# Attention with a gated FFN on one Trainium2 core: one half of scores in each block of six key tiles is exponentiated by GpSimd as a power of e^(1/4)

## The chip, the core and the metric

The kernel runs on one core of one Trainium2 chip. The engines are named as in the profile: PE is TensorE (PEld its weight loads), DVE is VectorE, ACT is ScalarE, POOL is GpSimd and SP is SyncE, which issues DMAs here. The metric is the device time of one execution in microseconds, as the median of several runs.

## The reference

All tensors are float32; the sequence has 2048 tokens of width 512. The input is normalised, and goes into an attention with 32 heads of width 16 and into a SwiGLU FFN of width 1792. The attention's output is multiplied by the SiLU of the FFN's output, and the input is added.

```python
def _A_ref(x, wqkv, wo):
    H = 32; Dh = D // H
    q, k, v = qkv[0], qkv[1], qkv[2]
    scale = Dh ** -0.5
    scores = jnp.einsum("bhqd,bhkd->bhqk", q, k) * scale
    p = _softmax(scores, axis=-1)
    o = jnp.einsum("bhqk,bhkd->bhqd", p, v)
    return (lambda x, *d: x.transpose(*d))(o, 0, 2, 1, 3).reshape(B, S, D) @ wo

def _B_ref(x, w_gate, w_up, w_down):
    g = _silu(x @ w_gate)
    u = x @ w_up
    return (g * u) @ w_down

xn = _layernorm(x, axis=-1)
s = _A_ref(xn, A_wqkv, A_wo)
g = _silu(_B_ref(xn, B_w_gate, B_w_up, B_w_down))
return x + s * g
```

The scale is 16^(-1/2) = 1/4, so the softmax needs exp(score / 4) of 32 x 2048 x 2048 scores.

## The kernel before

**Stages.** A prologue (to about 160 us) normalises the input and makes queries, keys and values. Then the attention and the FFN run interleaved for some 1,200 us, and the output projection ends the kernel.

**Units and blocks.** The attention goes through 32 units: 8 groups of four heads times 4 blocks of 512 queries. Each unit has 16 key tiles of 128 keys. `plan()` (L58) cuts these into 115 blocks of 2 to 6 key tiles, and says for each how many FFN steps stand behind each of its slots. 28 of the blocks have six key tiles and 24 FFN steps.

**Slots.** A key tile has two slots, `j` = 0 and 1, one for each pair of heads, so a block of six has 12 slots, n = 0 to 11. In a slot (L879 to L918) TensorE makes two products of 128 keys by 512 queries (L899), one for each head of the pair. They run side by side on two halves of the rows of the array. In a usual slot both land in the two halves of `score[j]` in PSUM, and one activation of 128x1024 takes the exponential of both into a tile `pr` (L902). In a slot that is `apart` the second half goes to the PSUM bank `spare`, of which there is only one. The slots in `shared` are apart, as is a block's last slot. For a block of six, `shared` is (2, 5, 7, 9, 11) and the FFN steps behind slots 2 to 11 are 1, 3, 3, 2, 3, 2, 2, 3, 1, 4. In a shared slot ScalarE exponentiates one half from PSUM (L910), and VectorE only copies the other half from PSUM to `pr` (L907). That copy goes on the list `kept_back`, and after the block's last slot ScalarE exponentiates all of the list in place (L920). So the five halves of a block of six that VectorE copies out are exponentiated late; the first of them is the second half of slot 2, which lies in the block's second key tile.

**Values.** Behind the first two slots of the next block, `values(prev)` (L418 to L424) multiplies the values with all of the last block's `pr`: four products for each key tile (L423), one for each head, key tile by key tile. TensorE takes its instructions in program order. So the values wait for each half's exponential in turn, and the rest of the block stands behind them.

**FFN steps.** `fill(n)` (L471) draws n steps from the generator `ffn` (L246). One step is a pair of products into the banks `bankx` and `banky` (L237). 24 steps make one tile of hidden features, and in the blocks of six they make exactly one. When a tile begins, behind slot 2, VectorE is given the split of the next gate and up weights into a high and a low part (`split_gu`, L198 a cast and L199 a subtraction, both from SBUF to SBUF), and a third of the way on the split of the next `w_down` rows (`split_wd`, L208 and L209, likewise). When it ends, ScalarE makes a tanh (L264), VectorE two products with it (L265 and L266), and then the split of the result (L230 and L231).

**Order.** The whole order is written out by hand (`tc.manual_schedule()`): each engine takes its instructions in program order, and semaphores are put in where data or buffers need them. GpSimd has constants and a few subtractions in the prologue, DMA issues in between (L243, L450), and two operations for each tile of the output from 1308 us on (`store_out`, L380 to L383, called from L398).

Of the kernel before, what the change touches and what calls it, by code (L numbers as in the profile page):

```python
# [2 lines left out]

# [6 lines left out]
F32 = mybir.dt.float32  # L10
# [3 lines left out]
AF = mybir.ActivationFunctionType  # L14
ALU = mybir.AluOpType
# [4 lines left out]
P = 128  # L20
# [6 lines left out]
TB = S // NB  # L27
# [14 lines left out]
SIZES = (2, 3, 4, 5, 6)  # L42
# [71 lines left out]
def tile_block(ctx: ExitStack, tc: tile.TileContext, x, wqkv, wo, w_gate, w_up, w_down, out):  # L114
# [3 lines left out]
    mm, act, dve, sp, pool = nc.tensor.matmul, nc.scalar.activation, nc.vector, nc.sync, nc.gpsimd  # L118
# [11 lines left out]
    const = ctx.enter_context(tc.tile_pool(name="const", bufs=1))  # L130
# [3 lines left out]

    ident = const.tile([P, P], F32, name="ident")
    make_identity(nc, ident)
    bankx = pone.tile([P, 512], F32, name="bankx")
    banky = pone.tile([P, 512], F32, name="banky")
    banks = (bankx, banky)
# [27 lines left out]
    def load_k(g, c, i=None):  # L167
        load_rows(kst[(g * NB + c) % RING if i is None else i],
                  k_d[:, g * 64:(g + 1) * 64, c * TB:(c + 1) * TB], KSLOT)

    def load_q(u, i=None):
        g, b = divmod(u, NB)
        load_rows(qst[u % 2 if i is None else i], q_d[:, g * 64:(g + 1) * 64, b * TB:(b + 1) * TB], QSLOT)

    def load_shift(u):
        for h in range(2):
            sp.dma_start(qst[u % 2][h * HALF:h * HALF + 2].bitcast(F32),
                         sh_d.rearrange("(s u) (j h t) -> u h s j t", s=2, j=2, h=2)[u, h])

    def load_v(g, c):  # L180
        sp.dma_start(vst[(g * NB + c) % RING], v_d[g][:, c * CT:(c + 1) * CT])
# [38 lines left out]
    def catch_up():  # L220
        while after:
            after.pop(0)()
# [135 lines left out]
    def out_steps():  # L358
        for b in range(NB - 1):
            if b not in stage and (len(queue) <= NB, 0 in stage and now > stage.get(0, now), ready[0] == DT)[b]:  # L360
                for c in range(DT - 1):
                    load_out(b, c)
                stage[b] = now
            if b in stage and b < 2 and (b, 1) not in stage and now > begin[u0 + b]:
                load_out(b, DT - 1)
                stage[b, 1] = now
            if b in stage and (b, 2) not in stage and now > stage[b] and (b < 2 or len(queue) <= 2):
                splits.extend((b, c) for c in range(DT - 1))
                stage[b, 2] = now
                for t in range(0 if b else NT):  # L370
                    load_gates(t)
            if (b, 1) in stage and (b, 5) not in stage and now > stage[b, 1]:
                splits.insert(0 if not b else len(splits), (b, DT - 1))
                stage[b, 5] = now
        for _ in range(min(2, len(splits))):
            b, c = splits.pop(0)
            split_o(lhs[b, c], parts_o[b, c])
            ready[b] += 1
# [39 lines left out]
    def values(item):  # L418
        u, tiles, probs = item
        for i, kt in enumerate(tiles):  # L420
            v = vst[(u // NB * NB + kt // CT) % RING]
            for h in range(4):
                mm(acc[h * 32:h * 32 + DH + 1], v[:, kt % CT, h * (DH + 1):(h + 1) * (DH + 1)],  # L423
                   probs[2 * i + h // 2][:, h % 2], start=kt == 0, stop=kt == KT - 1, skip_group_check=True)  # L424

    def turn_acc(first, last):
        o1 = late.tile([P, TB], F32, tag="o1", name="o1")
        dve.transpose(o1[:, :last - first], acc[:, first:last])
        return o1
# [13 lines left out]
    def finish(u, o1=None):  # L443
        g, b = divmod(u, NB)
        normalise(u, 0, TB, o1=o1)
        if g % 2:
            o2 = late.tile([P, TB], F32, tag="o1", name="o2")
            dve.transpose(o2, on[b])
            if g < NG - 1 or b < 2:
                (pool if g < NG - 1 else sp).dma_start(o_d[g // 2, b], o2)  # L450
            else:
                whole = hh.rearrange("p f j t -> p (f j) t")
                lhs[b, DT - 1] = whole[:, 2 * (DT - 1)], whole[:, 2 * DT - 1]
                split_o(lhs[b, DT - 1], o2)
                ready[b] += 1
# [15 lines left out]
    def fill(n):  # L471
        nonlocal given
        while n > 0 and not blocked():
            next(queue[0][1])
            queue[0][2] -= 1
            if not queue[0][2]:
                queue.pop(0)
            n -= 1
            given += 1
# [14 lines left out]
    with ExitStack() as pro:  # L494
# [53 lines left out]
        def low_w(m):  # L548
            hi, lo = parts_w(m)
            return pool.tensor_sub(lo, wraw[m], hi.bitcast(F32))  # L550
# [117 lines left out]
        for c in range(1, DT):  # L668
            high_w(8 + c)
            part = low_w(8 + c)  # L670
# [190 lines left out]
    exps = []  # L861

    coming = []
    for u in range(units):
        g, b = divmod(u, NB)
        q = qst[u % 2]
        kt = 0
        for now in range(begin[u], begin[u + 1]):
            size, shared, parts = blocks[now]
            ended, kept_back = None, []  # L870
            tiles = range(kt, kt + size)
            kt += size
            probs = []
            if not now:
                fill(FIRST[0])
            if now < 2:
                load_k(0, 2 + now)
                load_v(0, 2 + now)
            for n in range(2 * size):  # L879
                t, j = tiles[n // 2], n % 2  # L880
                if n == 2 and prev and prev[1][-1] == KT - 1:
                    values(prev)
                    if prev[0] < units - 2:
                        ended = prev[0]
                    else:
                        finish(prev[0])
                    catch_up()
                elif n == 2:
                    catch_up()
                    if prev:  # L890
                        values(prev)
                k, kc = kst[(g * NB + t // CT) % RING], t % CT


                room, last_pair = score[j], n == 2 * size - 1
                apart = last_pair or n in shared
                for h in range(2):
                    r = slice(h * HALF, h * HALF + NROW)
                    mm(spare if apart and h else room[:, h], k[r, j, kc * P:(kc + 1) * P], q[r, j], start=True, stop=True)  # L899
                pr = ppool.tile([P, 2, TB], F32, tag="pr", name="pr")  # L900
                if not apart:
                    exps.append(act(pr, room, AF.Exp, scale=0.25))  # L902

                for h in range(2) if apart else ():
                    src = spare if h else room[:, 0]
                    if n in shared and h != last_pair:
                        dve.tensor_copy(pr[:, h], src)  # L907
                        kept_back.append(pr[:, h])
                    else:
                        exps.append(act(pr[:, h], src, AF.Exp, scale=0.25))  # L910
                if n == 1 and now:
                    tc.add_manual_dep(exps[-1].ins, exps[-3].ins.name, settled, reason="order of the slots' writes")
                probs.append(pr)
                if ended is not None and n == max(2, 2 * size - 3):
                    o1 = turn_acc(0, TB)
                if ended is not None and last_pair:
                    finish(ended, o1)
                fill(parts[n])  # L918
            for part in kept_back:
                exps.append(act(part, part, AF.Exp, scale=0.25))  # L920
            if prev and prev[0] // NB + 1 < NG and prev[0] % NB == NB - 1:
                done = prev[1][-1] + 1
                while len(coming) < done // CT:
                    load_k(prev[0] // NB + 1, len(coming))
                    load_v(prev[0] // NB + 1, len(coming))
                    coming.append(now)
                if done == KT:
                    coming.clear()
            prev = u, tiles, probs
            if now == begin[u] + (not u) and u + 1 < units:  # L930
                load_q(u + 1)
                load_shift(u + 1)
            out_steps()
            if now == begin[units - 1] + 1:
                load_gate()
            if 0 <= now - begin[units - 1] - 3 < EARLY:
                gate_rest(now - begin[units - 1] - 3)
# [43 lines left out]
    part = low(1)  # L981
# [35 lines left out]
```

## Time and profile before

| | |
|---|---|
| median of 3 runs | 1396.76 us (1396.65 to 1397.27) |
| span of the profiled execution | 1394.9 us |
| PE busy | 1388.4 us |
| ACT busy | 1108.9 us |
| DVE busy | 689.8 us |
| POOL busy | 89.5 us |

The profile shows one execution. Its span is taken from the first to the last instruction, and the runs' times hold some 1.9 us more. A group's row reads: line, engine, operation, output and inputs by the program's names, shapes and count, then the busy time in us and the mean of one in ns, then the engine's idle time just before them. In the order of time a row has the start and the duration in us, and in brackets the idle time before it and what ended it. Matmuls are pipelined and their ends are modelled, so a busy PE is not PE at its peak.

### The profile page before, as it was taken

How to read it: one execution, taken by the hardware profiler on the slowest of the kernel's cores; microseconds unless marked ns; L12 is line 12 of the kernel's file. 1: busy time of each engine (PE TensorE's matmuls, PEld its weight loads, DVE VectorE, ACT ScalarE, POOL GpSimd, SP SyncE). 2: the span in 40 equal slices, each digit the busy share in tenths (PEclk: the TensorE clock that was granted, in tenths of full speed). 3: DMA queues.
4: the chain of work that ended last, by engine and by line, in shares of the span. 5: the costliest groups of instructions: out<-in, count | busy, mean ns of one | idle time of the engine just before them, and what ended most of it. 6: DMA issues, size and time to landing. Idle time of an engine off the chain costs nothing.

```text
span 1394.9 us, 27065 instructions
## 1 busy us (share of the span) xinstructions
PE 1388.4 (100%) x11197; PEld 835.5 (60%) x11197; DVE 689.8 (49%) x1126; ACT 1108.9 (79%) x1516; POOL 89.5 (6%) x102
## 2 busy tenths in 40 slices
PE   9999999999999999999999999999999999999998
PEld 7788655556555655565565555656556556555554
DVE  5643454254534563455356434644455434554645
ACT  6733587888888888888888888888888888888774
POOL 4200100000000000000000000000000000000254
PEclk9999999999999999999999999999999999999999
DMA  7778541134453511245533302257234302233642
GB/s 237 263 250 268 144 115 43 35 69 111 107 129 81 134 43 36 51 103 111 128 83 102 98 13 51 67 134 156 65 81 113 79 15 59 61 83 105 196 151 107
DMA packets 128687, 149.16 MB, mean 107 GB/s; under 512 B 12593, under 2 KB 80689, under 8 KB 127790
## 3 DMA queue, kind: packets, MB, share of 16 engines
q1 hardware_dynamic: 123246, 126.72, 36.1%
q0 software_dynamic: 4880, 20.12, 3.9%
q8 instruction: 89, 1.46, 0.5%
q10 hardware_dynamic: 432, 0.52, 0.1%
q14 instruction: 40, 0.33, 0.1%
HBM read 107.46 MB, written 40.11 MB: 106 GB/s over the span
## 4 chain that ended last, share of the span: by engine, by line
PE 87%; ACT 1%; DVE 1%; issue 0%; DVEq 0%; ACTq 0%
PE acc L423 32%; PE bankx L237 29%; PE score L899 18%; PE banky L237 7%; PE spare L899 1%; ACT pr L902 0%; PE spare L955 0%; PE banky L955 0%; PE score L955 0%; DVE hh L231 0%; DVE pr L907 0%; DVE gul L199 0%; ACT pr L910 0%; DVE hh L230 0%; DVE y L962 0%
## 5 line engine op out<-in xcount | busy, mean ns | idle before, releaser
L902 ACT ACTIVATE pr<-score 128x1024 f32<-128x1024 f32 x743 | 722.5, 1029 | 95.8 <-PE score L899 86.2
L423 PE MATMUL acc<-pr,vst 128*17 128x512 f32 x4096 | 461.8, 593 | 0.0
L899 PE MATMUL score<-qst,kst 50*128 50x512 f32 x1767 | 406.9, 407 | 0.4 <-ACT pr L902 0.4
L237 PE MATMUL bankx<-fx,guh 64*128 64x512 f32 x896 | 303.3, 392 | 0.2 <-PEq L810 0.2
L237 PE MATMUL banky<-fx,guh 64*128 64x512 f32 x896 | 303.2, 392 | 0.0
L899 PEld LDWEIGHTS score<-qst,kst 50*128 50x128 f32 x1767 | 193.3, 184 | 161.9 <-ACT pr L902 66.0
L423 PEld LDWEIGHTS acc<-pr,vst 128*17 128x17 f32 x4096 | 110.3, 97 | 280.4 <-issue 272.3
L907 DVE COPY pr<-spare 128x512 f32<-128x512 f32 x166 | 114.3, 689 | 249.5 <-PE spare L899 188.5
L910 ACT ACTIVATE pr<-score 128x512 f32<-128x512 f32 x221 | 131.7, 596 | 100.2 <-PE spare L899 72.2
L237 PE MATMUL bankx<-wd,hh 64*128 64x512 f32 x672 | 197.1, 392 | 0.0
L237 PE MATMUL banky<-wd,hh 64*128 64x512 f32 x672 | 197.1, 392 | 0.0
L237 PEld LDWEIGHTS bankx<-fx,guh 64*128 64x128 f32 x896 | 167.0, 187 | 26.7 <-issue 0.9
L237 PE MATMUL banky<-fx,gul 64*128 64x512 f32 x448 | 175.3, 391 | 0.0
L237 PE MATMUL bankx<-fx,gul 64*128 64x512 f32 x448 | 175.3, 391 | 0.0
L237 PEld LDWEIGHTS banky<-fx,guh 64*128 64x128 f32 x896 | 167.1, 187 | 3.2
L265 DVE SCALAR_TENSOR_TENSOR ga<-th,bankx 128x512 f32<-128x512 f32 x56 | 38.5, 687 | 201.4 <-ACT th L264 201.4
L237 PEld LDWEIGHTS bankx<-wd,hh 64*128 64x128 f32 x672 | 125.2, 186 | 18.6
L237 PEld LDWEIGHTS banky<-wd,hh 64*128 64x128 f32 x672 | 125.2, 186 | 5.9
L920 ACT ACTIVATE pr<-pr 128x512 f32<-128x512 f32 x226 | 124.2, 633 | 0.0
L899 PE MATMUL spare<-qst,kst 50*128 50x512 f32 x281 | 118.0, 420 | 0.2 <-DVE pr L907 0.2
L237 PEld LDWEIGHTS bankx<-fx,gul 64*128 64x128 f32 x448 | 83.0, 185 | 13.5
L237 PEld LDWEIGHTS banky<-fx,gul 64*128 64x128 f32 x448 | 83.0, 185 | 1.6
(171 smaller groups left out, 1400.8 us busy)
## 6 DMA issues: line engine op xcount, KB each, us to landing
gur<-in_B_w_gate_dram SPq DMA_DIRECT2D x56, 256.0 KB
gur<-in_B_w_up_dram SPq DMA_DIRECT2D x56, 256.0 KB
wdr<-in_B_w_down_dram SPq DMA_DIRECT2D x56, 256.0 KB
kst<-k_d SPq DMA_DIRECT2D x192, 64.0 KB
qst<-q_d SPq DMA_DIRECT2D x192, 64.0 KB
fx<-xt_d SPq DMA_DIRECT2D x24, 512.0 KB
q_d<-parts SPq DMA_DIRECT2D x16, 512.0 KB
k_d<-parts SPq DMA_DIRECT2D x16, 512.0 KB
```

What stands on the lines that cost most here:

```text
L237: mm(bank, lhs[h], rhs[h], start=start, stop=stop)
L265: dve.scalar_tensor_tensor(ga, th, 1.0, bankx, op0=ALU.add, op1=ALU.mult)
L423: mm(acc[h * 32:h * 32 + DH + 1], v[:, kt % CT, h * (DH + 1):(h + 1) * (DH + 1)], probs[2 * i + h // 2][:, h % 2], start=kt == 0, stop=kt ...
L899: mm(spare if apart and h else room[:, h], k[r, j, kc * P:(kc + 1) * P], q[r, j], start=True, stop=True)
L902: exps.append(act(pr, room, AF.Exp, scale=0.25))
L907: dve.tensor_copy(pr[:, h], src)
L910: exps.append(act(pr[:, h], src, AF.Exp, scale=0.25))
L920: exps.append(act(part, part, AF.Exp, scale=0.25))
```

## The change

A column `root4` of e^(1/4) is made once by VectorE. At the end of a block of six, the first entry of `kept_back`, which is the second half of slot 2, is no longer given to ScalarE. GpSimd raises `root4`, read along the row as a broadcast, to the power of that half, in place: (e^(1/4))^s = exp(s / 4). The other four entries, and all entries of smaller blocks, stay with ScalarE. There are 28 such powers.

```diff
+import math
...
     ident = const.tile([P, P], F32, name="ident")
     make_identity(nc, ident)
+    root4 = const.tile([P, 1], F32, name="root4")
+    dve.memset(root4, math.exp(0.25))
...
-            for part in kept_back:
-                exps.append(act(part, part, AF.Exp, scale=0.25))
+            for i, part in enumerate(kept_back):
+                if size == SIZES[-1] and not i:
+                    pool.tensor_tensor(part, root4.to_broadcast([P, TB]), part, op=ALU.pow)
+                else:
+                    exps.append(act(part, part, AF.Exp, scale=0.25))
```

`SIZES[-1]` is 6, `P` is 128 and `TB` is 512. The lines behind the first hunk move on by three in the changed kernel (L920 becomes L926).

## The prediction

> **What bounds the kernel now.** I read the busy shares first, then the chain that ended last, then the list of waits, and last the order of time inside one block of six key tiles.
>
> ```profile
> span 1394.9 us, 27065 instructions
> PE 1388.4 (100%) x11197; PEld 835.5 (60%) x11197; DVE 689.8 (49%) x1126; ACT 1108.9 (79%) x1516; POOL 89.5 (6%) x102
> PE 87%; ACT 1%; DVE 1%; issue 0%; DVEq 0%; ACTq 0%
> ```
>
> TensorE is busy for 1388.4 of 1394.9 us, and 87% of the chain that ended last is TensorE. ScalarE, from which the change takes work, is busy for 79% and holds 1% of the chain. So work taken off ScalarE pays only where TensorE waits for it. The waits of TensorE and of its weight loads on these exponentials are:
>
> ```profile
> PEld acc L423 <- ACT pr L920: 4.4, 18, 0.3
> PE score L899 <- ACT pr L902: 0.4, 1, 0.4
> PE spare L899 <- DVE pr L907: 0.2, 1, 0.2
> ```
>
> The columns are the total in us, the count and the longest. All that the late exponentials (L920) cost is 4.4 us in 18 weight loads. I take 4 us as the gain if nothing else happens, and 0 and 4.4 us as its bounds. Two neighbouring blocks show where ScalarE is tight:
>
> ```profile
> 436.58:449.14 12.56, 12.56 (x111) 7.41 (x109) 5.35 (x8) 9.94 (x14) 0.00 (x0) 1.00 0.31 85
> 449.14:462.27 13.13, 13.13 (x114) 7.72 (x112) 8.62 (x13) 10.12 (x15) 0.00 (x0) 1.00 0.27 66
> ```
>
> The columns are the stretch, its length, then the busy time of PE, PEld, DVE, ACT and POOL. The second row is a block of six: VectorE is busy for 8.62 us of 13.13 there, against 5.35 us in the block of five before it; TensorE is full in both. GpSimd is idle. The order on VectorE inside that block decides the case:
>
> ```profile
> 454.12 0.69 DVE L907 COPY pr<-spare 128x512 f32<-128x512 f32 x1 [1.79 <-PE spare L899]
> 454.73 0.68 DVE L198 CAST guh<-gur 128x1024 fp32r<-128x1024 f32 x1
> 455.44 1.23 DVE L199 TENSOR_TENSOR gul<-gur,guh 128x1024 fp32r<-128x1024 f32 x1
> 456.59 0.68 DVE L907 COPY pr<-spare 128x512 f32<-128x512 f32 x1
> 457.19 0.42 DVE L208 CAST wd<-wdr 128x512 fp32r<-128x512 f32 x1
> 457.64 0.69 DVE L209 TENSOR_TENSOR wd<-wdr,wd 128x512 fp32r<-128x512 f32 x1
> 458.25 0.68 DVE L907 COPY pr<-spare 128x512 f32<-128x512 f32 x1
> ```
>
> The first row is the copy of slot 2, the half that GpSimd is to exponentiate. Right behind it, with no gap, stand the cast and the subtraction that split the next gate weights, and behind these the copy of slot 5, which empties the bank `spare` for slot 7. TensorE needs that bank here:
>
> ```profile
> 457.64 0.39 PE L899 MATMUL spare<-qst,kst 50*128 50x512 f32 x1
> 462.27 1.48 PE L423 MATMUL acc<-pr,vst 128*17 128x512 f32 x12
> ```
>
> The copy of slot 5 ends at 456.59 + 0.68 = 457.27, and the product of slot 7 starts at 457.64: VectorE has 0.37 us to spare in the whole stretch.
>
> **The change, part by part.** *Removed:* 28 of the 226 late activations of L920, one in each of the 28 blocks of six.
>
> ```profile
> L920 ACT ACTIVATE pr<-pr 128x512 f32<-128x512 f32 x226 | 124.2, 633 | 0.0
> ```
>
> 28 x 633 ns = 17.7 us of ScalarE's time, of which at most the 4.4 us above stood in TensorE's way: minus 4 us. *Added once:* a memset of one column, some 0.1 us on VectorE before the input has landed: nothing. *Order:* TensorE, VectorE and SP keep their order; on GpSimd the 28 powers stand among DMA issues that nothing near needs. In one block (the 49th) an issue that waits for VectorE's transposes at the block's end stands ahead of the power; there the values wait for the power itself, some D + 0.5 us, and I count it like the others.
>
> *Added:* 28 powers on GpSimd, 128x512 from two SBUF inputs. No row shows a power. The nearest row is a GpSimd multiplication of the same shape, 1.27 us (below), so D, the time of one power, is at least 1.27 us. Upwards, a power is a logarithm, a product and an exponential. If it takes twenty elementary steps and each costs as much as that whole row, D is 25.4 us. I take 6 us: nearer to the row it resembles in shape and operands than to the far end, since steps on data already read need not be read and written again. This is the weakest number here.
>
> What does a power do to VectorE while it runs? The output stage has the same constellation, a GpSimd operation on two SBUF tiles that is released while VectorE runs a cast with a subtraction behind it:
>
> ```profile
> 1308.52 0.42 DVE L329 CAST wd<-wd 128x512 fp32r<-128x512 f32 x1
> 1308.97 1.68 DVE L330 TENSOR_TENSOR wd<-wd 128x512 fp32r<-128x512 f32 x1
> 1310.58 1.51 DVE L329 CAST wd<-wd 128x512 fp32r<-128x512 f32 x1
> 1312.13 0.69 DVE L330 TENSOR_TENSOR wd<-wd 128x512 fp32r<-128x512 f32 x1
> ...
> 1308.83 1.27 POOL L381 TENSOR_TENSOR y<-y,fx 128x512 f32<-128x512 f32 x1 [14.14 <-ACT pr L902]
> 1310.18 1.62 POOL L382 TENSOR_TENSOR pair<-y,pair 128x512 f32<-128x512 f32 x1
> ```
>
> GpSimd came during the cast and went first: the subtraction, 0.69 us when alone (last DVE row), took 1.68 us and ended at 1310.65, 0.55 us after GpSimd's end at 1310.10. The next cast took 1.51 us in place of 0.42 and ended 0.29 us after GpSimd's next end. So VectorE's work from SBUF to SBUF stands still for as long as GpSimd reads. What comes from PSUM doesn't: this transpose kept its 0.7 us under a running GpSimd operation.
>
> ```profile
> 1343.25 0.72 DVE L428 STREAM_TRANSPOSE o<-acc 128x512 f32<-128x512 f32 x1 [0.81 <-PE acc L423]
> 1342.53 1.28 POOL L381 TENSOR_TENSOR y<-y,fx 128x512 f32<-128x512 f32 x1 [1.80 <-DVE y L397]
> ```
>
> The Trainium skill, "SBUF — State Buffer", section "Who interferes with whom", says that a GpSimd operation which gets the shared pair of SBUF ports first keeps it for the whole instruction, and that a VectorE instruction with two SBUF inputs fully blocks. By it a slow power holds VectorE as completely as a quick product does; no run so far shows this for a power.
>
> Put into the block: the copy of slot 2 ends at 454.81, so the power arrives during the cast (until 455.41), as GpSimd's product did. It goes first and ends about D - 0.14 us after the cast (a product that met a cast and took 1.27 us ran on after it for 1310.10 - 1308.94 = 1.16, or 0.11 less; I take 0.14, which is also what a subtraction saves behind a GpSimd operation, 0.69 - 0.55). The subtraction ends at the power's end plus 1.23 - 0.14 = 1.09 us, at 456.36 + D, where it ended at 456.67. VectorE is late by D - 0.31 us. (The last block of six has no weights left to split; there the cast of `wd` behind slot 5 is the first to be held.) What waits behind it is the copy of slot 5, and for that TensorE at slot 7, in order, with all fills and scores behind it. With 0.37 us to spare, TensorE stands still for S = D - 0.68 us in each block: 5.3 us for D = 6. The values of that block don't wait for the power a second time, since they shift by S too and stood 462.27 - 455.41 = 6.9 us behind the cast.
>
> A stall of this length has a second price. At the end of the kernel the granted clock (third column from the right) fell soon after the last product:
>
> ```profile
> 1389.94 0.40 PE L955 MATMUL banky<-fx,rl 128*128 128x512 f32 x1
> 1392.00:1393.00 1.00, 0.00 (x0) 0.00 (x0) 0.00 (x0) 0.00 (x0) 0.00 (x0) 0.96 0.62 217
> 1393.00:1394.00 1.00, 0.00 (x0) 0.00 (x0) 0.00 (x0) 0.00 (x0) 0.00 (x0) 0.50 0.19 66
> ```
>
> 0.96 over the one us and 0.50 in the next: the clock halved at 1392.9, some 2.6 us after the product ended at 1390.34. How long it takes to come back is seen at the start:
>
> ```profile
> 1.07 5.06 PE L555 MATMUL extra<-busy 128*128 128x128 f32 x22 [1.07 <-DVE ind L562]
> 6.57 0.42 PE L611 MATMUL extra<-ident,xn 128*128 128x128 f32 x1
> 6.78 0.42 PE L611 MATMUL banky<-ident,xn 128*128 128x128 f32 x1
> 9.67 0.60 PE L611 MATMUL extra<-ident,xn 128*128 128x128 f32 x4
> ```
>
> Transposes are 0.21 us apart until 6.78, and at 9.67 four fit into 0.60 us. At half speed for 6.78 - 1.07 = 5.7 us, TensorE lost 2.9 us. I take 2.9 us for each stall over 3 us (bounds 0, if the clock holds through such a stall, and 2.9). "TensorE: Matmul & The Clock Gate", section "Part 1: The HAM clock gate", in the Trainium skill gives a free-running window of 3.4 us both ways; by that estimate the price is 1.7 to 3.4 us, or 48 to 95 us in all.
>
> *Sum* for D = 6 us: 28 x (5.3 + 2.9) = 230, less 4: plus 226 us. The profiled execution becomes 1394.9 + 226 = 1621 us; the median stands 1396.8 - 1394.9 = 1.9 us above this span, so **1623 us**. By the bounds of D: 1.27 us gives 28 x 0.59 - 4 = plus 13 (1409 us), 25.4 us gives 28 x (24.7 + 2.9) - 4 = plus 769 (2166 us).
>
> **The rivals.** *The power is short* (D under 2.5 us): the stall is at most 1.8 us, the clock stays up, and the time lies between 1409 and 1443 us. For it speaks the shape of the row, against it that a power is no single operation. 11%.
>
> *The power is very long* (D over 18 us): over 1397 + 28 x (17.3 + 2.9) - 4 = 1958 us. Nothing in the trace excludes it. 11%.
>
> *The other side: the power does not hold VectorE.* If GpSimd takes its 512 columns in pieces and computes with the ports free, the subtraction slips in. Then the power is hidden as long as it ends before the values need it, 7 us behind the cast (462.27 and one product), and TensorE loses its waits for L920: 1396.8 - 4 = 1393 us. It decides up to D = 7 us. The rows of the output stage speak against it, but only for operations whose time is reading. 12%.
>
> *Not held, but late:* with D over 7 us, the values wait instead, 28 x (D - 7) us; 28 x 3 = 84, or 1477 us for D = 10. 6%.
>
> **How the numbers follow.** The forecast, a held VectorE with D between 2.5 and 18 us, has 60%; its own range is 1443 to 1958 us. The range leaves out the very long power, and takes in the rest: 1391 to 1950 us. This kernel can tell about 0.2%, 2.8 us, from no change. Of the 12% for the free VectorE I count 9 as over 2.8 of at most 4.4 us and 3 as less; one more falls to no change from the late powers just past 7 us. So faster 0.09, same 0.04, slower 0.87.
>
> **What would show it.** In the changed profile, the mean of the new GpSimd group is D. Right: the subtraction L199 (now three lines on) in blocks of six takes about D + 1 us and ends 1.1 us after the power; TensorE's idle time names VectorE's copy of `spare` as its releaser, 28 times; ScalarE's late group counts 198; the granted clock falls below 0.95 on average. Wrong: the subtraction keeps 1.23 us while a power runs; or the releaser of the values is GpSimd; or the clock stays at 1.00 across stalls of 5 us, which would take up to 81 us off. The size of D alone moves the time by 28 us for each us.

## The result, and the profile after

The changed kernel takes 3540.11 us (median of 4 runs, 3538.12 to 3544.52) against 1396.70 us before: 2.53 times as long, with a 95% interval of 2.531 to 2.538. The forecast was 1623 us in a range of 1391 to 1950 us. The direction was right, the size was not.

The page of the changed kernel: busy shares, the chain that ended last, and the two costliest groups.

```profile
span 3539.5 us, 27132 instructions
PE 1495.2 (42%) x11197; PEld 844.1 (24%) x11197; DVE 709.6 (20%) x1127; ACT 1095.6 (31%) x1488; POOL 2392.6 (68%) x130
POOL 65%; PE 26%; issue 4%; DVE 1%; ACT 0%; DVEq 0%; POOLq 0%; ACTq 0%
L924 POOL TENSOR_TENSOR pr<-root,pr 128x512 f32<-128x512 f32 x28 | 2302.5, 82233 | 660.1 <-DVE pr L910 660.1
L426 PE MATMUL acc<-pr,vst 128*17 128x512 f32 x4096 | 552.4, 660 | 2036.4 <-POOL pr L924 2036.4
```

GpSimd went from 89.5 us of work to 2392.6 us, and now holds 65% of the chain. One power takes 82.2 us: that is 65 times the GpSimd product of the same shape (1.27 us). TensorE is idle for 2036 us in front of the values (L426), and what ends that idle time is the power. The list of waits of the changed kernel (total in us, count, longest) says the same for the weight loads, which come first:

```profile
PEld acc L426 <- POOL pr L924: 2062.2, 28, 82.7
PE acc L426 <- POOL pr L924: 2036.4, 28, 81.7
```

28 waits for 28 powers. The order of time in the first of these blocks shows what each engine does (start and duration in us; first VectorE, then GpSimd, then TensorE's values):

```profile
170.39 0.68 DVE L910 COPY pr<-spare 128x512 f32<-128x512 f32 x1
171.00 0.68 DVE L201 CAST guh<-gur 128x1024 fp32r<-128x1024 f32 x1
171.71 1.94 DVE L202 TENSOR_TENSOR gul<-gur,guh 128x1024 fp32r<-128x1024 f32 x1
173.58 0.68 DVE L910 COPY pr<-spare 128x512 f32<-128x512 f32 x1
174.18 0.41 DVE L211 CAST wd<-wdr 128x512 fp32r<-128x512 f32 x1
174.63 0.69 DVE L212 TENSOR_TENSOR wd<-wdr,wd 128x512 fp32r<-128x512 f32 x1
...
171.23 82.27 POOL L924 TENSOR_TENSOR pr<-root,pr 128x512 f32<-128x512 f32 x1 [6.69 <-DVE pr L910]
...
179.21 1.89 PE L426 MATMUL acc<-pr,vst 128*17 128x512 f32 x10
253.56 2.77 PE L426 MATMUL acc<-pr,vst 128*17 128x512 f32 x12 [72.46 <-POOL pr L924]
```

The power runs from 171.23 to 253.50. VectorE is held only at its start: the subtraction of the gate weights takes 1.94 us in place of 1.23 and is done at 173.65. The next cast and subtraction, both from SBUF to SBUF, take their usual 0.41 and 0.69 us while the power runs. The rest of the block runs on and TensorE starts the values at 179.21. Each product of the values has two rows in the trace (4096 rows for 2048 products), so the ten rows are the four products of the first key tile and the first of the second. The sixth product needs the half that GpSimd has not finished, and there TensorE stands for 72 us. So the forecast had the wrong place for the stall too: not at slot 7 behind VectorE, but at the values behind GpSimd.

The clock in the same stretch (the stretch and its length, busy time of PE, PEld, DVE, ACT and POOL with counts, granted clock, DMA share, GB/s):

```profile
182.00:186.00 4.00, 0.00 (x0) 0.00 (x0) 0.14 (x1) 1.34 (x2) 4.00 (x1) 0.99 0.59 131
186.00:253.50 67.50, 0.00 (x0) 0.00 (x0) 0.00 (x0) 0.00 (x0) 67.50 (x1) 0.50 0.00 0
253.50:257.50 4.00, 3.94 (x20) 0.85 (x24) 0.00 (x0) 0.00 (x0) 0.00 (x1) 0.50 0.02 4
257.50:261.00 3.50, 3.50 (x32) 1.31 (x26) 0.49 (x1) 0.53 (x1) 0.00 (x0) 0.99 0.00 0
```

It is halved by 186, some 5 us into the stall, and stays so for 4.0 us after the power has ended; that costs some 2.0 us of TensorE's work. The mean granted clock of the whole execution is 0.71.

### The profile page after: what moved, and what is told of

Read it like the earlier page. It is cut to its first block, busy times and chain, and to the rows that moved or that the text cites. A ratio compares the mean times of both kernels' runs of the same rounds, so it can differ in the third digit from the quotient of the medians.

```text
span 3539.5 us, 27132 instructions
## 1 busy us (share of the span) xinstructions
PE 1495.2 (42%) x11197; PEld 844.1 (24%) x11197; DVE 709.6 (20%) x1127; ACT 1095.6 (31%) x1488; POOL 2392.6 (68%) x130
## 4 chain that ended last, share of the span: by engine, by line
POOL 65%; PE 26%; issue 4%; DVE 1%; ACT 0%; DVEq 0%; POOLq 0%; ACTq 0%
POOL pr L924 65%; PE acc L426 12%; PE bankx L240 7%; PE score L902 5%; PE banky L240 1%; DVE pr L910 0%; ACT pr L905 0%; PE spare L902 0%; PE spare L961 0%; PE banky L961 0%; POOL o_d L453 0%; DVE o L431 0%; DVE o L451 0%; DVE hh L234 0%; PE score L961 0%
## 5 line engine op out<-in xcount | busy, mean ns | idle before, releaser
L924 POOL TENSOR_TENSOR pr<-root,pr 128x512 f32<-128x512 f32 x28 | 2302.5, 82233 | 660.1 <-DVE pr L910 660.1
L426 PE MATMUL acc<-pr,vst 128*17 128x512 f32 x4096 | 552.4, 660 | 2036.4 <-POOL pr L924 2036.4
L426 PEld LDWEIGHTS acc<-pr,vst 128*17 128x17 f32 x4096 | 117.8, 105 | 2399.9 <-POOL pr L924 2062.2
L902 PE MATMUL score<-qst,kst 50*128 50x512 f32 x1767 | 415.9, 409 | 0.4 <-ACT pr L905 0.4
L902 PEld LDWEIGHTS score<-qst,kst 50*128 50x128 f32 x1767 | 201.3, 184 | 153.7 <-issue 67.2
L431 DVE STREAM_TRANSPOSE o<-acc 128x512 f32<-128x512 f32 (+1 forms) x33 | 22.9, 695 | 1009.3 <-PE acc L426 1009.3
L246 POOL DMA_DIRECT2D g_d<-y x16 | 8.8, 553 | 170.6 <-DVE y L245 156.9
L926 ACT ACTIVATE pr<-pr 128x512 f32<-128x512 f32 x198 | 109.7, 634 | 0.0
```

The source lines that it names most:

```text
L246: pool.dma_start(g_d[r:r + P], y)
L924: pool.tensor_tensor(part, root4.to_broadcast([P, TB]), part, op=ALU.pow)
```

## The experiments

Two theories stood against each other after the result. *Held* is the forecast's: VectorE stands still for as long as the power runs. *Late* is the one that the trace suggests: GpSimd reads its inputs quickly and computes with VectorE free, and the values wait for the result. All edits below are made in the changed kernel.

**64 columns.** GpSimd gets only 64 of the 512 columns of the half.

```diff
-                    pool.tensor_tensor(part, root4.to_broadcast([P, TB]), part, op=ALU.pow)
+                    pool.tensor_tensor(part[:, :64], root4.to_broadcast([P, 64]), part[:, :64], op=ALU.pow)
+                    exps.append(act(part[:, 64:], part[:, 64:], AF.Exp, scale=0.25))
```

> GpSimd raises only the first 64 columns of the half; ScalarE exponentiates the other 448. In the changed kernel 512 columns took 82.2 us, 160.6 ns each, so the power should take about 10.3 us plus a fixed part. Theory 'late' (GpSimd reads its inputs quickly and computes with VectorE free; the next block's values wait for the power): the values stand about 7 us behind it, so TensorE waits 3.3 to 3.6 us in each of 28 blocks, 92 to 101 us, and at most 2.9 us a block more for the clock (81 us): 1489 to 1579 us, the waits named as weight loads of the values on GpSimd. Rival 'held' (the forecast: VectorE stands still for the whole power): S = D - 0.68 = 9.8 us and 2.9 us for the clock: 1397 + 28 x 12.7 = 1753 us, with VectorE's subtraction of the gate weights at some 11 us.

One run: 1484.6 us against 1397.1 us before, a little under the band of *late* and 268 us under *held*. The group and the waits:

```profile
L924 POOL TENSOR_TENSOR pr<-root,pr 128x64 f32<-128x64 f32 x28 | 304.1, 10862 | 625.2 <-DVE pr L910 625.1
PEld acc L426 <- POOL pr L924: 81.2, 28, 11.3
```

10.86 us for 64 columns. The 27 ordinary waits come to (81.2 - 11.3) / 27 = 2.6 us each, and 81.2 us of waits make up nearly all of the 87.5 us. A weight load waits longer than TensorE is idle, since the products before it, by their modelled ends, are still running: by the row `PE acc L426 <- POOL pr L924: 55.5, 28, 10.4` TensorE itself stands still for (55.5 - 10.4) / 27 = 1.7 us in an ordinary block. The mean clock of the run is 0.995, so these stalls do not halve it. One wait is 11.3 us long, as long as the whole power; that is the 49th block, of which the next run tells more. VectorE's subtraction of the gate weights keeps its 1.23 us in this run (mean of all 56): no hold can be seen with 64 columns.

**32 columns.** The same with 32 columns, so that the power ends before the values need it.

> The same with 32 columns on GpSimd and 480 on ScalarE: the power should take 5.1 to 5.5 us. Theory 'late': it ends before the values need it, no wait for GpSimd remains, and only the reading of 32 columns can hold VectorE (about 0.1 us): 1393 to 1399 us. Rival 'held': S = 4.6 us, 28 x 4.6 = plus 129 us without and plus 210 us with the clock: 1526 to 1607 us.

Measured: 1406.35 us, ratio 1.0064 (1.0047 to 1.0081). *Held* is out by more than 100 us, but the time is also 9.3 us over the kernel before, where *late* had expected nothing. The group, the waits and a part of the chain that ended last between 745 and 775 us (start and duration):

```profile
L924 POOL TENSOR_TENSOR pr<-root,pr 128x32 f32<-128x32 f32 x28 | 160.5, 5732 | 664.8 <-DVE pr L910 664.8
PEld acc L426 <- POOL pr L924: 6.2, 1, 6.2
...
746.15 0.59 POOL o_d L453
746.76 5.45 POOL pr L924
752.26 7.28 PE acc L426 x38
```

One wait is left of 28. It is that of the 49th block: there the power stands in GpSimd's queue behind a DMA issue of L453, which waits for VectorE's last transpose, and starts at 746.76, after the block. 38 instructions of the values take 7.28 us right behind it where 40 take 4.42 us elsewhere in the kernel before: the granted clock is 0.50 from 752 to 757 us.

**32 columns, but not in the 49th block.** The power's condition is given `and now != 48`.

> As e_cols32, but the 49th block, where the power stands behind a DMA issue of GpSimd that waits for VectorE's last transpose of the block, keeps ScalarE's exponential. Theory 'the 9.3 us of e_cols32 are that one block: the power begins at the block's end, the values wait some 6 us, and the clock halves once': 1396 to 1398 us. Rival 'a third of a us is lost in each of the blocks': 1406 us as before.

Measured: 1397.19 us, ratio 1.0001 (0.9992 to 1.0011), which cannot be told from before. So the 9.3 us were that one block: some 6 us of waiting and the rest the clock. A power of this length that is early enough costs nothing that these runs can tell.

**64 columns that nobody reads.** ScalarE does all exponentials as before the change; GpSimd makes a power of a constant at the same moment, into a tile of its own.

```diff
+    junk = const.tile([P, 64], F32, name="junk")
...
-                        dve.tensor_copy(pr[:, h], src)
+                        copies.append(dve.tensor_copy(pr[:, h], src))
...
                 if size == SIZES[-1] and not i:
-                    pool.tensor_tensor(part, root4.to_broadcast([P, TB]), part, op=ALU.pow)
-                else:
-                    exps.append(act(part, part, AF.Exp, scale=0.25))
+                    made = pool.tensor_tensor(junk, root4.to_broadcast([P, 64]), root4.to_broadcast([P, 64]), op=ALU.pow)
+                    tc.add_manual_dep(made.ins, copies[0].ins.name, settled, reason="at the time of the copy")
+                exps.append(act(part, part, AF.Exp, scale=0.25))
```

`copies` is a new list of VectorE's copies in the block, in order; the added dependence lets the power start when the first of them, that of slot 2, is done.

> ScalarE exponentiates every half as before the change; GpSimd makes a power of 64 columns of a constant into a tile that nobody reads, released by the same copy of slot 2. It takes the same 10.3 us, but no one waits for its result. Theory 'late': nothing is left of the 92 us and more of the run in which 64 columns are read: 1396 to 1401 us. Rival 'held' or any other disturbance by a running GpSimd (ports, memory): the same 1753 us as forecast for it there, or at least tens of us.

Measured: 1396.56 us, ratio 0.9996 (0.9986 to 1.0005), with the powers as long as before:

```profile
L925 POOL TENSOR_TENSOR junk<-root 128x64 f32<-128x64 f32 x28 | 303.2, 10829 | 569.3 <-DVE pr L911 569.2
```

303 us of GpSimd work beside the blocks, and no loss. So the 87.5 us of the first experiment come from the wait for the result and what follows on it, and not from a GpSimd at work. The power also takes the same time on a constant as on the scores (10.83 and 10.86 us).

**A multiplication in place of the power.** `op=ALU.mult`, all 512 columns. It leaves the exponential of these halves out.

> The power is replaced by a multiplication of the same operands, 128x512 in place (these 28 halves then carry no exponential: that part of the computation is left out). Duration 1.27 to 1.6 us, as the other GpSimd products of this shape. Theory 'late': the result is there long before the values; what remains is VectorE's subtraction, held while GpSimd reads, about 0.7 us as in the changed kernel (1.94 in place of 1.23 us), less 0.37 us to spare: 28 x 0.35 = 10 us, 1400 to 1410 us. The forecast's own formula S = D - 0.68 gives 28 x 0.59 - 4: 1409 us. Rival 'the operation itself costs nothing in arithmetic, the wait is for any GpSimd result': thousands of us as in the changed kernel.

Measured: 1417.03 us, ratio 1.0144 (1.0127 to 1.0160): 20 us over before, 7 us over the upper end of what was expected. Here the wait for the power is gone and the hold is left. VectorE and GpSimd in one block:

```profile
343.01 0.68 DVE L201 CAST guh<-gur 128x1024 fp32r<-128x1024 f32 x1
343.73 1.94 DVE L202 TENSOR_TENSOR gul<-gur,guh 128x1024 fp32r<-128x1024 f32 x1
345.60 0.68 DVE L910 COPY pr<-spare 128x512 f32<-128x512 f32 x1
...
343.18 1.42 POOL L924 TENSOR_TENSOR pr<-root,pr 128x512 f32<-128x512 f32 x1 [38.47 <-DVE pr L910]
```

The subtraction takes 1.94 us behind a product of 1.42 us, and the same 1.94 us behind a power of 82.27 us. The product ends at 344.60 and the subtraction 1.07 us later, so a product holds VectorE to its own end, as the forecast read from the output stage; the power of the same operands holds it no longer than the product does. With 512 columns of these operands the hold is 0.71 us, whichever of the two is computed.

TensorE pays for it at the bank `spare`. The waits of its weight loads on VectorE's copy (total in us, count, longest) in the kernel before, here, and in the changed kernel are:

```profile
PEld spare L899 <- DVE pr L907: 1.1, 2, 0.6
PEld spare L902 <- DVE pr L910: 22.0, 49, 1.3
PEld spare L902 <- DVE pr L910: 21.9, 48, 1.3
```

The 20 us are these waits, and the changed kernel has them too.

**The multiplication, released by the copy of slot 7.** By then VectorE has made both splits, and has only copies from PSUM until the block ends.

```diff
...
-                    pool.tensor_tensor(part, root4.to_broadcast([P, TB]), part, op=ALU.pow)
+                    made = pool.tensor_tensor(part, root4.to_broadcast([P, TB]), part, op=ALU.mult)
+                    tc.add_manual_dep(made.ins, copies[2].ins.name, settled, reason="after the splits")
```

`copies` is made as in `e_unread64`; its third entry is the copy of slot 7.

> As e_mult (a multiplication in place of the power), but released by the copy of slot 7 and so behind both splits of weights, where VectorE has only copies from PSUM until the block's end. Theory 'GpSimd holds VectorE only for SBUF inputs, while it reads': the 20 us of e_mult vanish, and the time is that of e_none, 1392 to 1397 us. Rival 'a GpSimd product of this size costs some 0.7 us a block wherever it stands': 1410 to 1417 us.

Measured: 1399.63 us, ratio 1.0020 (1.0010 to 1.0030). 17 of the 20 us are gone, and the subtraction is back at 1.23 us; the product now lies beside copies from PSUM (VectorE, then GpSimd):

```profile
340.25 1.23 DVE L202 TENSOR_TENSOR gul<-gur,guh 128x1024 fp32r<-128x1024 f32 x1
344.39 0.69 DVE L910 COPY pr<-spare 128x512 f32<-128x512 f32 x1 [0.65 <-PE spare L902]
...
343.82 1.04 POOL L924 TENSOR_TENSOR pr<-root,pr 128x512 f32<-128x512 f32 x1 [38.04 <-DVE pr L910]
...
PEld acc L426 <- POOL pr L924: 1.8, 1, 1.8
```

The 2.8 us that are left were expected to be nothing. The last row above, from the list of waits, accounts for 1.8 us of them: one wait for GpSimd's product, and it is that of the 49th block, where the product starts behind a DMA issue again. The other 1 us stays open. The product itself takes 1.04 us here (mean of 28) against 1.35 us in `e_mult`: where VectorE reads SBUF at the same time, GpSimd's product is slowed as well.

**Nothing at all.** In blocks of six the first late half gets no exponential on any engine (`continue` in place of the power), which leaves that part of the computation out.

> In blocks of six the first late half gets no exponential at all, on any engine (that part of the computation is left out); ScalarE has 28 x 0.63 us less to do and GpSimd nothing more. It bounds what the change could bring if the power were free. By the waits of the kernel before (4.4 us of weight loads on L920): 1392 to 1395 us. Rival 'ScalarE binds these blocks': 28 x 0.63 = 17.7 us, 1379 us.

Measured: 1396.60 us, ratio 0.9997 (0.9988 to 1.0006): no change. The waits for the late exponentials are gone from the list, and the time is the same. So a power that cost nothing would have brought nothing that can be told from the kernel before.

**128 columns.**

> 128 columns on GpSimd. By e_cols32 (5.73 us) and e_cols64 (10.86 us) a power takes 0.6 us and 160.3 ns a column: 21.1 us here. Theory 'late': the values wait some 13.5 us in each of 28 blocks, 378 us; the hold by reading 128 columns is nothing; the clock, which stayed up through the 3 us stalls of e_cols64, halves in each block and takes back 2.3 us as in the changed kernel (64 us): 1830 to 1845 us. Without the price of the clock: 1775 us. Rival 'held': 28 x (20.4 + 2.9): 2049 us.

One run: 1826.0 us, 4 us under the band of *late* with the clock, 51 us over it without, 223 us under *held*.

```profile
L924 POOL TENSOR_TENSOR pr<-root,pr 128x128 f32<-128x128 f32 x28 | 589.0, 21034 | 659.2 <-DVE pr L910 659.1
PEld acc L426 <- POOL pr L924: 364.6, 28, 21.5
```

429 us more than before are 365 us of waits and 64 us besides; the mean clock of this run is 0.902. VectorE's subtraction is hardly held (1.26 us, mean of all 56, against 1.23).

## Why the prediction was wrong, step by step

*What bounds the kernel* was read rightly: TensorE, with ScalarE's late exponentials off the path. *The gain of 4 us* was still too much. The 4.4 us of weight loads that waited for L920 cost no time: `e_none` takes them away and changes nothing. In their place more weight loads of the values wait for nothing that the profile names ("issue": 876 waits and 272.3 us in the kernel before, 903 and 280.8 us in `e_none`), about 0.3 us each in both.

Two steps failed. The first, and the one that put the time outside the range, is *the time of one power*. It was "the weakest number here": 6 us, with bounds of 1.27 and 25.4 us; it is 82.2 us. The rival of a very long power (D over 18 us) was given 11%, and the range left it out. The four sizes lie on a line:

| columns | mean of one, us | us a column against the size above |
|---|---|---|
| 32 | 5.73 | |
| 64 | 10.86 | 0.160 |
| 128 | 21.03 | 0.159 |
| 512 | 82.23 | 0.159 |

So a power costs 0.16 us a column and some 0.6 us once. The product of 512 columns that the prediction started from costs 1.27 us, 0.0025 us a column: the power is no chain of twenty such steps, but as dear as some 65 of them. Against the product of its own operands, 1.04 us in `e_mult_late`, the power is 79 times as dear. The upper bound was an assumption about how a power is made, and no row stood behind it.

The second step that failed is *the hold of VectorE*, and with it S = D - 0.68. The order was as forecast: the power comes during the cast, goes first, and the subtraction waits. But the subtraction is longer by only 0.71 us, at 1.94 us behind the power and behind the product alike. The prediction took the operations of the output stage, which hold VectorE to their end, and carried "for as long as GpSimd reads" over to "for as long as the power runs". The Trainium skill ("SBUF — State Buffer", "SBUF: two separate sides") says that whichever starts first, a GpSimd operation or a VectorE operation with two SBUF inputs, gets the pair of ports for the whole instruction. For the power the runs show otherwise: VectorE's casts and its subtractions of two SBUF inputs ran at full speed inside 80 us of it. That GpSimd takes in all its operands first and computes from its own memory would explain this; the trace shows that VectorE is free, not that memory. The size of D alone would not have mended the forecast: with D = 82.23 its own sum gives 1397 + 28 x (81.55 + 2.9) - 4 = 3758 us, 218 us over the measured time, and puts the stall in the wrong place.

*The 0.37 us to spare* were read at slot 7 alone. With a product the formula gave plus 13 us, and the run 20 us. The later slots have less room. In the block of `e_mult` shown above, the products of slots 5, 7, 9 and 11 into `spare` start at 344.26, 346.33, 347.99 and 349.50; in the kernel before they start at 340.90, 342.56, 343.96 and 345.42. So they come 3.36, 3.77, 4.03 and 4.08 us later: slot 7 loses 0.41 us, slot 9 another 0.26 and slot 11 another 0.05, and the hold of 0.71 us is lost as a whole. The 26 blocks in which the subtraction is held lose 18.0 us, and the 49th block's queue comes on top.

*The stall* was put at slot 7, with VectorE's copy as the releaser of TensorE. The long one stands at the values, with GpSimd as the releaser; at slot 7 and behind it only the short waits for the hold are found. The rival "not held, but late", given 6%, named the mechanism: 28 x (D - 7) with D = 82.23 is 2106 us. The waits measured are 2062 us. The whole difference of the two spans is 3539.5 - 1394.9 = 2144.6 us: 2062 us of waits, 20 us for the hold (the spans of `e_mult` and the kernel before, 1415.3 - 1394.9), and 62 us left over.

*The clock* was right in kind and a little too dear: those 62 us are 2.2 us a block against 2.9 forecast. The clock's own record agrees: after the ends of the 28 powers it stays at 0.50 for 2.6 to 6.0 us, 126 us in all, and half of that is lost. The spread has a pattern. The stretches at half speed around the stalls last 71.68 or 75.09 us in the changed kernel (81.92 in the 49th block), 10.24 or 13.65 us with 128 columns (20.48 in the 49th block) and 6.83 us in the one stall with 32: all multiples of 3.41 us. The limit of 3 us for a stall fits the runs, but not as a sharp one: idle times of TensorE of some 1.7 us (64 columns) left the clock up, one of 5.3 us (the 49th block of 32 columns) halved it, and in the longer stalls the clock fell 2.1 to 5.4 us after TensorE's last product. Nothing between 1.8 and 5.3 us was run. The window of 3.4 us in the Trainium skill ("TensorE: Matmul & The Clock Gate", "Part 1: The HAM clock gate") agrees with these stretches and stalls, and the 1.7 to 3.4 us that the prediction estimated from it hold the 2.2.

*The 49th block* was told rightly, at D + 0.5 us: the longest wait of the changed kernel is 82.7 us. With 32 columns it was all of the loss that was left.

No experiment points to a version that beats both kernels. With the power shrunk to what fits, the time is that of before, and `e_none` shows that there is nothing to win on this path.

## What to carry to other kernels

Before work is moved to an idle engine, time that one operation there at its real size: where no row shows it, the range should not end at a guess about its inner steps. Then ask two separate questions about the engine that shares its ports, how long it is held and who needs the result at what time, and look through the moved work's queue for the one place where something in front of it is late. A wait on the list is no gain until a run without its cause is faster.

## What was not expected of the hardware

A GpSimd power of float32 costs 0.16 us for each column of 128 partitions, the same from 32 to 512 columns. It shares SBUF with VectorE much better than its length suggests: VectorE's subtraction lost 0.7 us to 82 us of it, and nothing to one of 64 columns (`e_cols64`, `e_unread64`).
